# A new hand-written order table for a two-layer attention and gated-MLP kernel: zero products chained and fewer, MLP loads queued behind the query-weight transposes

## The chip, the cores and the metric

The kernel runs on one core of one Trainium2 chip. The metric is the device time of one execution in microseconds. Three timed runs of the kernel before gave 378.32, 379.09 and 379.13 us; the median, 379.09 us, is the number that the change is measured against.

## The reference, cut to what matters

`x` is 2048 x 512 in bfloat16. Two identical layers follow each other; each is an attention block with a softmax feature map instead of a softmax over positions (32 heads of 16), and then an MLP whose gate is rectified.

```python
def _A_ref(x, wqkv, w_phi, wo):
    q, k, v = split_heads(x @ wqkv)                          # 32 heads x 16
    pq, pk = q @ w_phi, k @ w_phi                            # per head
    phi = lambda p: concat([softmax(p), softmax(-p)])        # 32 features
    kv, z = phi(pk).T @ v, sum over positions of phi(pk)
    o = (phi(pq) @ kv) / (phi(pq) @ z + 1e-6)
    return merge_heads(o) @ wo
def _B_ref(x, W_gate, W_up, W_down):                         # 512 -> 1376 -> 512
    gate = x @ W_gate
    return (gate * (gate > 0) * (x @ W_up)) @ W_down
for layer in range(2):
    x = x + _A_ref(layernorm(x), ...)
    x = x + _B_ref(layernorm(x), ...)
```

The point that shapes the schedule: `kv` and `z` are sums over all 2048 positions, so no position's attention output can start before the keys of every position are done.

## The kernel before, in words

The 2048 rows are 16 tiles of 128, in four chunks of four. x stays in SBUF (tile `X`) and is updated in place; the output goes out tile by tile at the end.

**Start.** SP issues the loads of X tiles 0 and 1 (`LOAD_SP`); ACT issues the feature weights `wf`, the key half of `wkv`, X tiles 2 to 7 and the value half (`LOAD_ACT`), and later X tiles 8 to 15 and the query weights `wq` (`LATE`, L226 to L234). The MLP's and the output projection's weights (`st.loads`, L213 to L218) are 28 loads on SP (L238). `wake` (L250) issues products of a zero tile on TensorE (PE, line L256); nothing reads their results. `feature_weights` (L260) folds the per-head matrix `w_phi` into the key weights (PE transposes at L289, PE products at L302, evacuations at L245 or L247) and into the query weights. The query weights are transposed by two DMA transposes that SP issues (L275), which wait for `wq`.

**Per tile, attention.** `Norm` (L308 on) makes the layernorm: DVE statistics (L326, L328), small POOL operations (L334, L336, L384, L386), the normalised tile on ACT, POOL or DVE (L398, L410), then its transpose, either on PE (L419) with an evacuation, or by a DMA transpose on SP (L424 for two tiles, L428 for one). `keys_values` (L635 on) does, per tile: four PE products with the folded key weights (L648, called "k" below), two exponentials on ACT (L669), four PE products for the values (L601, "v") and an evacuation (L245 or L247); sums of the exponentials on DVE, partly halved first on POOL (L617, L620, L626, L630), a reciprocal (L678), the scaling of the features split between POOL and DVE (L683), and eight small PE products that add the tile to `kv` (L706, "s"). When all 16 tiles are added, `build_R` (L728, DVE, two operations) makes the matrix R. `queries` (L735 on) does the same for the queries (L748, "q"; ACT L752; DVE L757; POOL or DVE L761, L768; DMA transpose L770). The queries of the first three chunks do not need R; those of the fourth wait for the sums (`gate` is 3). `attention` (L775 on) multiplies by R on PE (L787, "a"), divides on DVE (L805, L807), transposes (PE L827 or SP) and projects with `wo` (L838, "p"), and DVE adds to X (L504).

**Per chunk, MLP.** `glu` (L513 on) has gate and up products (L551, "g", with the remainder columns at L531), ACT and DVE for the gating (L557, L561, L564, L568), and the products with `wd` (L583, "d"), which DVE adds to X (L508). In the first layer every tile that is finished goes through `Norm` again and through `keys_values` of the second layer.

**What sets the order.** Every operation is first recorded by `pl.op`, and gets a number in the order of recording. Then `Plan.order` takes the operations in the sequence of the table `ORDER`, and each engine executes its own operations strictly in that sequence. The durations and arrival times written beside an operation (`at`, `lat`, `WK_IN`, `X_IN`) are for the table's maker; they emit nothing. Inside `reads` and `writes`, a key that is not a buffer (such as `("wqin", 0)`) only demands that the table has the one operation behind the other; the waits on the chip come from the data that the instructions touch. So the table decides three things: the sequence of each engine, the sequence of SP's and ACT's DMA issues, and which buffer an operation gets. `STEP` holds the choices per tile: which engine evacuates, normalises or scales (A is ACT, D is DVE, P is POOL).

Decoded, TensorE's sequence in the table of before begins so (z is a zero product, w and wq the folding of the key and query weights, n a PE transpose of a normalised tile, the number behind a letter the tile; "0" for the layer is left out):

```
zx11 wx4 n0 w zx2 wx3 clear z n1 zx3 k0 k1 zx2 n2 v0 n3 k2 z k3 v2 n6 n7 v1 v3 n4 n5 k6 wq k4
v5 k5 wqx2 k7 wq k8 k9 zx2 q4 q0 s0 v4 q1 q6 s0 v6 v8 z s1 k11 q11 s2 v7 s3x2 k10 s4 q2 s5 k13
v13 s5 s6 q3 v11 k14 k15 v14 s7 v15 v9 k12 s7 v10 s8 v12 s8 q7 q5 q8 s9x2 s10 s11 q10 s11 s12
s13 s14x2 s15 q13 z a0 z q15 z p0 a1 q12 p0 p1 q9 a2 ...
```

and around the passage to the second layer (a digit 1 ahead of the colon is that layer):

```
... 1:k10 1:v2 1:v1 d15 d12 d14 d13 1:q6 1:v3 1:s0x2 1:v6 1:s1x2 1:k15 1:v10 1:v7 1:v5 1:v9 1:k12
1:v4 1:k14 1:s2 1:k13 1:s3x2 1:v8 1:v12 1:s4x2 1:s5x2 1:s6x2 1:s7 1:v15 1:v13 1:s7 1:v11 ...
```

SP's sequence begins: one load of `wu`, the two transposes of `wq`, the transposes of X tiles 8 and 9, then seven loads, and so on.

Of the kernel before, what the change touches and what calls it, by code (L numbers as in the profile page):

```python
# [121 lines left out]
WF_IN, WK_IN, WV_IN, WQ_IN, LOADED = 3.5, 5.92, 10.8, 14.7, 13.0  # L122
X_IN = [3.25, 4.0] + [8.06] * 2 + [9.5] * 4 + [12.1] * 4 + [13.4] * 4
# [102 lines left out]
def load_weights(st):  # L226

    nc, seen = st.nc, {}
    st.pl.rank("xl")
    before = ()  # L230
    for what, issue in st.late:
        keys = [("wqin", 0)] if what == "q" else [("Xin", t) for t in range(*what)]
        st.pl.op("ACT", 0.45, issue, reads=list(before), writes=keys, at=3.6, lat=2.0)
        before = keys[:1]  # L234
    for n, (name, dst, src, kb) in enumerate(st.loads):
        i = seen[name] = seen.get(name, -1) + 1
        st.pl.rank("ld" if name == "wd" else "l", n)
        st.pl.op("SP", 0.475, lambda dst=dst, src=src: nc.sync.dma_start(out=dst, in_=src), writes=[(name, i)], at=LOADED, lat=2.2, tx=kb / 245.0)  # L238
# [11 lines left out]
def wake(st):  # L250

    nc, pl = st.nc, st.pl
    pl.rank("z")
    for i in range(STEP["wake"]):
        z = Buf("ps", [P, D], F32)
        pl.op("PE", 0.2155, lambda z=z: nc.tensor.matmul(z[:], lhsT=st.zero[:, 0:P], rhs=st.zero[:], start=True, stop=True),  # L256
              writes=[(z, 0)], at=1.2)


def feature_weights(st):  # L260
# [8 lines left out]
    for name, dst, off, at in (("Wk2", st.Wk2, D, WK_IN), ("Wq2", st.Wq2, 0, WQ_IN)):  # L269
        pl.rank("w" if off else "wq")  # L270
        by_dma = not off
        if by_dma:
            wt = [Buf("b2", [P, 2, NDB, P], BF16) for m in range(2)]
            for m in range(2):
                pl.op("SP", 1.34, lambda m=m: nc.sync.dma_start_transpose(  # L275
                    out=wt[m][:].rearrange("p m b c -> p (m b) c"), in_=st.wq[:, 2 * m:2 * m + 2, :].rearrange("p m d -> p (m d)")),
                    reads=[("wqin", 0)], writes=[(wt[m], 0)], at=at, lat=1.88)
# [317 lines left out]
def values(st, t, ti, xnT, L):  # L595
# [7 lines left out]
    pl.op("PE", 4 * MM, mm, reads=[(xnT, ti)], writes=[(vp, 0)], at=WV_IN, group=("v" + L, t))  # L603
# [131 lines left out]
def queries(st, c, xnT, L, after=()):  # L735
    nc, pl = st.nc, st.pl
    pT = []
    for ti in range(TPC):
        t = c * TPC + ti
# [11 lines left out]
        for s in range(2):  # L751
# [10 lines left out]
              reads=[(sq2, 0), (sq2, 1)], writes=[(rq, 0)], port=not by_pool)  # L762
# [12 lines left out]
def attention(st, c, pT, norm, L):  # L775
# [73 lines left out]
    "turn": "DAADDAAD", "wake": 26, "fuse0": "AFAA", "fuse1": "FFFF", "gate": 3, "sA": 3, "xB0": "ADAADDDADDDAAAAA",  # L849
# [162 lines left out]
```

## Time and profile before

| | |
|---|---|
| three timed runs | 378.32, 379.09, 379.13 us; median 379.09 us |
| the profiled execution | 380.21 us |
| its span, first to last instruction | 378.5 us |
| what lies around the span | 1.71 us |
| mean granted TensorE clock | 0.995 |
| busy: PE, PEld, DVE, ACT, POOL | 369.6, 197.4, 263.8, 211.0, 137.5 us |

PEld is the loading of weights into TensorE, which goes on beside the products. A line of a timeline gives start, duration, engine, line, operation, output and input tile, and count; in square brackets stands how long the engine stood idle before it, and what ended that wait. A line of a table by stretches gives the stretch, its length, the busy time of each engine with the number of instructions, the granted TensorE clock (1.00 is full speed), the busy share of the DMA engines and GB/s. A line of the chain of waits gives start, duration and what. All times are microseconds from the start of the span. Buffer numbers are left out of tile names, so `ps` is any of the six PSUM buffers and `b` any of the SBUF work buffers.

### The profile page before, as it was taken

The page shows a single profiled execution, that of the slowest core. Times are in us where ns is not written, and L with a number is a line of the kernel's source. Part 1 is how long each engine was busy: PE and PEld are TensorE (multiplying, and loading weights), DVE is VectorE, ACT ScalarE, POOL GpSimd, SP SyncE. Part 2 cuts the span into 40 slices and gives each one's busy share as a digit, 9 for nine tenths or more (in the row PEclk, how much of TensorE's full clock was granted, in tenths as well). Part 3 has the DMA queues.
Part 4 walks back from the last instruction along what each step waited for, and adds up shares of the span by engine and source line. Part 5 has one row for each costly group of instructions (what it writes and reads, how often), then busy time and mean ns, then how long its engine had stood idle before and what let it go on. Part 6 is the DMA issues. An engine that isn't in the chain of part 4 may idle for free.

```text
span 378.5 us, 6950 instructions
## 1 busy us (share of the span) xinstructions
PE 369.6 (98%) x2536; PEld 197.4 (52%) x2536; DVE 263.8 (70%) x610; ACT 211.0 (56%) x476; POOL 137.5 (36%) x223
## 2 busy tenths in 40 slices
PE   7999998999999999999999999999999999999996
PEld 3454545867655444444444446476555544444453
DVE  6998998999896695535585876899846535434432
ACT  4999995967657525865587175686531342232100
POOL 5899996453330005410745257245200100100000
PEclk9999998999999999999999999999999999999999
DMA  8766385659864203600250062157851513201021
GB/s 273 178 172 140 86 206 122 130 92 142 119 136 71 57 8 65 133 5 2 56 99 0 5 100 38 29 103 136 156 84 55 72 40 44 70 0 16 0 66 61
DMA packets 95746, 31.83 MB, mean 84 GB/s; under 512 B 87424, under 2 KB 95200, under 8 KB 95712
## 3 DMA queue, kind: packets, MB, share of 16 engines
q1 hardware_dynamic: 93024, 27.97, 38.5%
q10 hardware_dynamic: 2688, 3.42, 2.6%
q8 instruction: 20, 0.33, 0.4%
q14 instruction: 14, 0.11, 0.1%
HBM read 8.44 MB, written 2.10 MB: 28 GB/s over the span
## 4 chain that ended last, share of the span: by engine, by line
PE 82%; DVE 8%; POOL 5%; DMA 3%; issue 1%; ACT 0%; ACTq 0%; POOLq 0%
PE ps L551 37%; PE ps L583 20%; PE ps L838 7%; PE ps L748 5%; PE ps L648 3%; PE ps L531 3%; PE q L787 2%; PE ps L601 2%; DVE b L683 2%; POOL b L683 2%; DMA wkv<-in_A_wqkv_dram 1%; DVE sk L630 1%; DMA b<-b 1%; POOL b L617 1%; PE q L706 1%
## 5 line engine op out<-in xcount | busy, mean ns | idle before, releaser
L551 PE MATMUL ps<-b,wg 128*128 128x512 bf16 (+3 forms) x440 | 81.8, 321 | 0.0
L551 PE MATMUL ps<-b,wu 128*128 128x512 bf16 (+3 forms) x440 | 81.3, 321 | 0.0
L561 ACT ACTIVATE b<-ps 128x512 bf16<-128x512 f32 (+3 forms) x110 | 50.4, 484 | 54.5 <-PE ps L551 53.5
L583 PE MATMUL ps<-wd,b 128*128 128x512 bf16 (+4 forms) x374 | 79.1, 366 | 0.0
L564 DVE SCALAR_TENSOR_TENSOR b<-ps,b 128x512 bf16<-128x512 f32 (+2 forms) x60 | 34.1, 593 | 32.4 <-PE ps L551 17.1
L583 PEld LDWEIGHTS <-b 128*128 128x128 bf16 (+1 forms) x374 | 35.5, 98 | 39.5
L551 PEld LDWEIGHTS <-wg 128*128 128x128 bf16 x440 | 38.8, 98 | 31.7
L551 PEld LDWEIGHTS <-wu 128*128 128x128 bf16 x440 | 38.0, 98 | 29.2
L683 POOL TENSOR_TENSOR b<-b,rk 128x1024 bf16<-128x1024 bf16 (+6 forms) x26 | 37.2, 1443 | 22.3 <-ACT sq L486 12.7
L617 POOL TENSOR_TENSOR b<-b 128x256 f32<-128x256 bf16 x39 | 26.9, 695 | 39.0 <-ACT b L752 23.0
L669 ACT ACTIVATE b<-ps 128x512 bf16<-128x512 f32 x64 | 36.8, 640 | 7.5 <-PE ps L648 6.8
L752 ACT ACTIVATE b<-ps 128x512 bf16<-128x512 f32 x64 | 35.1, 617 | 10.2 <-PE ps L748 6.8
L748 PE MATMUL ps<-Wq,b 128*128 128x512 bf16 x128 | 32.7, 386 | 0.0
L648 PE MATMUL ps<-Wk,b 128*128 128x512 bf16 x128 | 32.0, 379 | 0.3 <-DMA b<-b 0.3
L838 PE MATMUL ps<-wo,b 128*128 128x512 bf16 x128 | 32.2, 379 | 0.0
L601 PE MATMUL ps<-wkv,b 128*128 128x512 bf16 x128 | 31.2, 379 | 0.0
L504 DVE SCALAR_TENSOR_TENSOR X<-ps,X 128x512 bf16<-128x512 f32 x32 | 21.7, 684 | 10.0 <-PE ps L838 9.6
L508 DVE SCALAR_TENSOR_TENSOR X<-ps,r,X 128x512 bf16<-128x512 f32 (+2 forms) x22 | 15.1, 700 | 18.2 <-PE ps L583 18.2
L486 ACT ACTIVATE sq<-b 128x512 bf16<-128x512 bf16 x32 | 20.3, 633 | 13.5 <-DVE b L465 13.1
L490 POOL TENSOR_SCALAR ve<-tot 128x4 f32<-128x4 f32 x8 | 1.9, 233 | 65.0 <-ACT sq L486 65.0
L568 DVE TENSOR_TENSOR b<-b,b 128x128 bf16<-128x128 bf16 (+2 forms) x50 | 16.7, 361 | 11.5 <-ACT b L557 7.2
L557 ACT ACTIVATE b<-ps 128x128 bf16<-128x128 f32 (+2 forms) x50 | 20.6, 428 | 6.8 <-PE ps L551 6.1
(94 smaller groups left out, 507.1 us busy)
## 6 DMA issues: line engine op xcount, KB each, us to landing
out_dram<-X SPq DMA_DIRECT2D x15, 128.0 KB, 1.8
X<-in_A_x_dram ACTq DMA_DIRECT2D x3, 512.0 KB, 6.9
b<-b SPq DMA_TRANSPOSE x91, 3.1
wu<-in_B_W_up_dram SPq DMA_DIRECT2D x8, 160.0 KB, 4.1
wd<-in_B_W_down_dram SPq DMA_DIRECT2D x5, 256.0 KB, 4.3
wg<-in_B_W_gate_dram SPq DMA_DIRECT2D x8, 160.0 KB, 3.5
wkv<-in_A_wqkv_dram ACTq DMA_DIRECT2D x2, 512.0 KB, 6.4
wq<-in_A_wqkv_dram ACTq DMA_DIRECT2D x1, 512.0 KB, 4.8
```

What stands on the lines that cost most here:

```text
L551: nc.tensor.matmul(ps[:], lhsT=wt[:, b, f * P:(f + 1) * P], rhs=xnT[:, lo:hi, b, :], start=(b == 0), stop=(b == NDB - 1))
L561: pl.op("ACT", 0.045 + 0.43 * share, lambda ups=ups, ru=ru, sign=1.0 if fuse else -1.0: nc.scalar.activation(out=ru[:], in_=ups[:], func=A ...
L564: pl.op("DVE", 0.058 + 0.548 * share, dur=0.138 + 0.548 * share, fn=lambda gps=gps, ru=ru, h=h, cs=cs: nc.vector.scalar_tensor_tensor(out= ...
L583: nc.tensor.matmul(yps[:], lhsT=hs[f][:fsz, ti * P:(ti + 1) * P], rhs=st.wd[:fsz, f, cols], start=(f == 0), stop=(f == NFT - 1))
L601: nc.tensor.matmul(vp[:], lhsT=xnT[:, ti, kb, :], rhs=st.wkv[:, kb, D:2 * D], start=(kb == 0), stop=(kb == NDB - 1))
L617: nc.gpsimd.tensor_tensor(out=h[:].rearrange("p j h f -> p j f h"), in0=x[:, :, 0], in1=x[:, :, 1], op=Alu.add)
L648: nc.tensor.matmul(ps[:], lhsT=xnT[:, ti, kb, :], rhs=w(kb), start=(kb == 0), stop=(kb == NDB - 1))
L669: pl.op("ACT", 0.48, lambda s=s, ek=ek, pk=pk: nc.scalar.activation(out=ek[:, :, s, :], in_=pk[:].rearrange("p (j x) -> p j x", j=8), func ...
L683: eng.tensor_tensor(out=phiK[:, lo:hi, :, :].rearrange("p j s (f h) -> p (j s) f h", h=4), in0=ek[:, lo:hi, :, :].rearrange("p j s (f h) - ...
L748: nc.tensor.matmul(pq[:], lhsT=xnT[:, ti, kb, :], rhs=st.Wq2[:, kb, :], start=(kb == 0), stop=(kb == NDB - 1))
L752: pl.op("ACT", 0.48, lambda s=s, eq=eq, pq=pq: nc.scalar.activation(out=eq[:, :, s, :], in_=pq[:].rearrange("p (j x) -> p j x", j=8), func ...
L838: nc.tensor.matmul(yps[:], lhsT=turned(b), rhs=st.wo[:, b, :], start=(b == 0), stop=(b == NDB - 1))
```

## The change

The 28 weight loads move into a function of their own, which is recorded after `feature_weights`; each now has the key of the second query-weight transpose among its reads, so in any table they stand behind both transposes. The zero products are 20 instead of 26; each reads the key of the one before it, and the value products of the first four tiles read the key of the last, so that all zero products stand ahead of them. The transposed tile 0 of the first layernorm is evacuated by ACT instead of DVE (`turn`), and in `xA` (the norm ahead of the second layer) tiles 0, 7 and 10 go from DVE to ACT and tiles 2 and 8 from ACT to DVE. The estimates of arrival times are new, and one flag for the table's maker (`long`) is set on a POOL operation. The table `ORDER` is new.

```diff
-WF_IN, WK_IN, WV_IN, WQ_IN, LOADED = 3.5, 5.92, 10.8, 14.7, 13.0
-X_IN = [3.25, 4.0] + [8.06] * 2 + [9.5] * 4 + [12.1] * 4 + [13.4] * 4
+WF_IN, WK_IN, WV_IN, WQ_IN, LOADED = 3.5, 5.95, 10.0, 14.1, 13.0
+X_IN = [3.27, 3.85] + [7.2] * 2 + [8.5] * 4 + [11.4] * 4 + [12.8] * 4
...
+def later_loads(st):
+
+    nc, seen = st.nc, {}
     for n, (name, dst, src, kb) in enumerate(st.loads):
         i = seen[name] = seen.get(name, -1) + 1
         st.pl.rank("ld" if name == "wd" else "l", n)
-        st.pl.op("SP", 0.475, lambda dst=dst, src=src: nc.sync.dma_start(out=dst, in_=src), writes=[(name, i)], at=LOADED, lat=2.2, tx=kb / 245.0)
+        st.pl.op("SP", 0.475, lambda dst=dst, src=src: nc.sync.dma_start(out=dst, in_=src), reads=[("turned", 1)], writes=[(name, i)], at=LOADED, lat=2.2, tx=kb / 245.0)
...
-              writes=[(z, 0)], at=1.2)
+              reads=[("z", i - 1)] if i else [], writes=[(z, 0), ("z", i)], at=1.2)
...
-                    reads=[("wqin", 0)], writes=[(wt[m], 0)], at=at, lat=1.88)
+                    reads=[("wqin", 0)], writes=[(wt[m], 0), ("turned", m)], at=at, lat=1.88)
...
-    pl.op("PE", 4 * MM, mm, reads=[(xnT, ti)], writes=[(vp, 0)], at=WV_IN, group=("v" + L, t))
+    pl.op("PE", 4 * MM, mm, reads=[(xnT, ti)] + ([("z", STEP["wake"] - 1)] if L == "0" and t < 4 else []), writes=[(vp, 0)], at=WV_IN, group=("v" + L, t))
...
-    "turn": "DAADDAAD", "wake": 26, "fuse0": "AFAA", "fuse1": "FFFF", "gate": 3, "sA": 3, "xB0": "ADAADDDADDDAAAAA",
-    "xB1": "DDAAAAAAAADDDDAD", "xA": "DDAADDDDAADDADAD", "xm0": "11222111", "xmB0": "12221222", "xmB1": "22121122",
+    "turn": "AAADDAAD", "wake": 20, "fuse0": "AFAA", "fuse1": "FFFF", "gate": 3, "sA": 3, "xB0": "ADAADDDADDDAAAAA",
+    "xB1": "DDAAAAAAAADDDDAD", "xA": "ADDADDDADAADADAD", "xm0": "11222111", "xmB0": "12221222", "xmB1": "22121122",
...
+    later_loads(st)
```

The table's numbers are not comparable line by line, because the numbering moves: the loads are 3 to 30 before and 156 to 183 after, the first layernorm 31 to 135 before and 3 to 107 after, the zero products 136 to 161 before and 108 to 127 after, the folding 162 to 189 before and 128 to 155 after, and all the rest is 6 lower after. Decoded, TensorE's new sequence is

```
zx11 wx5 zx2 wx3 z n0 zx2 n1 zx2 k0 k1 n2 zx2 v0 clear k2 n3 v2 n6 v3 n4 n5 k3 n7 k4 wq k6 v1
wqx2 k5 wq k7 k9 v4 q0 v7 v5 q4 s0 k8 q1 s0 s1 q6 k10 v6 v8 q2 s2 s3 q3 k11 s3 k13 s4 s5x2 s6
s7 v9 k14 s7 s8x2 v11 v10 k15 v15 q11 k12 q10 v12 s9x2 v14 s10 v13 q5 q7 q8 s11x2 s12 s13
s14x2 s15 q13 a0 q15 p0 a1 q12 p0 p1 q9 a2 ...
```

and around the passage to the second layer

```
... d15 d14 1:v9 d12 1:v2 d13 1:v3 1:v6 1:s1 1:k15 1:v5 1:s1 1:v8 1:v4 1:k12 1:v11 1:k13 1:s2
1:s3x2 1:s4x2 1:v12 1:k14 1:s5x2 1:v13 1:v10 1:s6x2 1:s7 1:v15 1:s7 1:s8 1:v14 1:s9 ...
```

SP begins with the two transposes of `wq`, two loads, the transposes of X tiles 8 and 9, and four loads; at the passage it issues the DMA transposes of tiles 15, 12, 13, 14 (before: 15, 12, one of a query, 14, 13). ACT issues the load of `wq` behind the evacuations of tiles 0 and 1 (before: ahead of that of tile 1). On DVE's queue, 109 operations end with the last feature scaling of the first layer, where there were 111: the evacuation of tile 0 and one reciprocal of the queries (L757) are no longer among them. On POOL's queue, the operations up to its last such scaling are 66 instead of 67 (one L617 of the queries is behind it).

More of the change, by code (lines that the diff above doesn't have):

```diff
@@ L226, in load_weights @@
 def load_weights(st):
-    nc, seen = st.nc, {}
+    nc = st.nc
     st.pl.rank("xl")
@@ L761, in queries @@
               lambda sq2=sq2, rq=rq, e=nc.gpsimd if by_pool else nc.vector: e.tensor_tensor(out=rq[:], in0=sq2[:, :, 1, :], in1=sq2[:, :, 0, :], op=Alu.mult),
-              reads=[(sq2, 0), (sq2, 1)], writes=[(rq, 0)], port=not by_pool)
+              reads=[(sq2, 0), (sq2, 1)], writes=[(rq, 0)], port=not by_pool, long=by_pool)
         on_dve = STEP["qs" + L][t] == "D"
```

144 rows, old and new, of the table ORDER are left out of this document.

## The prediction

> **What bounds the kernel now.** I read the busy shares first, then the same by stretches of the run.
>
> ```profile
> PE 369.6 (98%) x2536; PEld 197.4 (52%) x2536; DVE 263.8 (70%) x610; ACT 211.0 (56%) x476; POOL 137.5 (36%) x223
> 20.00:30.00 10.00, 10.00 (x66) 5.10 (x64) 9.76 (x24) 10.00 (x22) 9.60 (x14) 1.00 0.75 188
> 55.57:58.98 3.41, 1.65 (x29) 1.02 (x28) 3.41 (x6) 2.45 (x6) 2.69 (x4) 1.00 0.67 210
> 58.98:62.40 3.42, 3.42 (x23) 1.74 (x24) 2.04 (x6) 1.04 (x2) 1.67 (x3) 0.50 0.71 165
> 64.00:216.60 152.60, 152.60 (x1010) 82.78 (x1007) 112.24 (x280) 96.71 (x239) 52.69 (x95) 1.00 0.40 71
> 216.60:240.00 23.40, 22.71 (x227) 12.50 (x226) 16.69 (x33) 13.63 (x26) 13.16 (x16) 1.00 0.34 58
> 240.00:375.70 135.70, 135.56 (x870) 71.72 (x867) 77.08 (x170) 49.05 (x115) 16.52 (x27) 1.00 0.33 63
> ```
>
> 98% for TensorE hides two regimes. Behind 64 us TensorE has no gap worth a name: whatever time the attention starts earlier, the end comes earlier, and whatever a new order makes it wait is added. Ahead of that DVE (9.76), ACT (10.00) and POOL (9.60 of 10.00 at 20 to 30) are as full as TensorE, and from 55.57 TensorE does 1.65 us of work in 3.41, while DVE is full. The chain of waits and the timeline say who leads there.
>
> ```profile
> 38.42 4.19 POOL L683 TENSOR_TENSOR b<-b,rk 128x768 bf16<-128x768 bf16 x3
> 56.01 2.89 DVE b L683 x3
> 58.94 0.62 PE L706 MATMUL q<-vext,b 128*128 128x68 bf16 x8 [0.81 <-DVE b L683]
> 59.38 1.90 PE L748 MATMUL ps<-Wq,b 128*128 128x512 bf16 x4
> 59.60 0.79 DVE L728 TENSOR_TENSOR R<-M,q 128x272 bf16<-128x272 bf16 x2
> 61.07 0.63 PE L256 MATMUL ps<-zero 128*128 128x512 bf16 x1
> 61.50 0.66 PE L787 MATMUL q<-R,b 128*128 128x68 bf16 x8
> 61.96 0.59 PE L256 MATMUL ps<-zero 128*128 128x512 bf16 x1
> 62.19 0.36 DVE L805 RECIPROCAL dd<-q 128x32 f32<-128x32 f32 x1 [1.26 <-PE q L787]
> 62.59 0.69 DVE L807 TENSOR_TENSOR b<-q,dd 128x512 bf16<-128x512 f32 x1
> 63.26 0.38 PE L256 MATMUL ps<-zero 128*128 128x512 bf16 x1
> 63.47 0.39 PE L827 MATMUL ps<-ident,b 128*128 128x128 bf16 x4
> 205.54 1.73 PE ps L601 x8
> ```
>
> POOL and then DVE scale the last keys (L683), TensorE adds them (L706), DVE builds R from 59.60 to 60.39. The first attention product could start then; it starts at 61.50, because one query group (L748, at half clock: 59.38 to the next start, 61.07, so 1.69; a full-speed group of four takes 0.865, half of the 1.73) and a zero product (61.07 to 61.50, 0.43) stand ahead of it. Three zero products lie on this path.
>
> **The change part by part.** *R.* Two instructions fewer stand on DVE's full queue ahead of the last scaling: tile 0's evacuation and one reciprocal.
>
> ```profile
> L247 DVE COPY b<-ps 128x512 bf16<-128x512 bf16 x7 | 2.6, 417 | 1.4 <-PE ps L289 1.2 <-PE ps L419 0.3
> L757 DVE RECIPROCAL sq<-sq 128x32 f32<-128x32 f32 x32 | 10.7, 339 | 0.1
> ```
>
> That is 0.417 + 0.339 = 0.76 us; POOL, the other full queue, has one L617 fewer there, so it follows. ACT takes the evacuation over, some 0.6 us, beside exponentials that it has to make anyway; if ACT leads in the first 20 us, half of the gain is gone. I take R 0.76 earlier, at 58.84.
>
> *The early load.* One load of `wu` no longer runs beside the key weights, whose arrival starts the work.
>
> ```profile
> 1.71 0.42 SPq L238 DMA_DIRECT2D wu<-in_B_W_up_dram  x1
> 6.79 1.07 PE L289 MATMUL ps<-ident,wkv 128*128 128x128 bf16 x16 [1.47 <-DMA wkv<-in_A_wqkv_dram]
> 5.00:6.00 1.00, 0.32 (x2) 0.00 (x0) 0.97 (x5) 0.00 (x0) 0.92 (x3) 1.00 1.09 368
> ```
>
> Its 160 KB at 368 GB/s are 0.43 us of engines that are full. How much of it lay ahead of the key weights the trace doesn't show: 0 to 0.43. I take 0, since the load was issued last of the three on SP; 0.43 goes into the range. The Trainium skill, DMA: Bandwidth & Descriptors, section Queues, rings and completion order, says that each DMA engine alternates between the queues packet by packet, so that SP's load would take turns with ACT's; the full DMA share in the row agrees, and by the rule alone the sum would be up to 0.43 better.
>
> *The other loads.* All 28 wait behind the transposes of `wq`, as 27 did before.
>
> ```profile
> 14.26 2.71 SPq L275 DMA_TRANSPOSE b<-wq  x2
> 59.52 0.45 SPq L238 DMA_DIRECT2D wu<-in_B_W_up_dram  x1
> wu<-in_B_W_up_dram SPq DMA_DIRECT2D x8, 160.0 KB, 4.1
> 69.22 0.61 PE L551 MATMUL ps<-b,wu 128*128 128x128 bf16 x8
> ```
>
> The last one was issued at 59.52 and landed some 4.1 later, at 63.6; the MLP starts at 69.22. The 5.6 us of cover make later issues free, also if `wq`, now issued behind two evacuations, comes a microsecond later and holds SP. Behind the waiting transposes stand only loads and the transposes of tiles 8 and 9, issued at 21.00 before. Cost 0; without cover, one for one.
>
> *The zero products.* Nine instead of 12 lie between 6.79 and R; these three stood in a stage that DVE and POOL bound, so I take 0, between 0 and 3 x 0.22 = 0.65. The three behind R go: the one at 61.07 gives 0.43. The other two stand where TensorE waits for DVE to divide: from 61.50 to the transpose at 63.47 are 1.97 us. Without them the path is the product 0.25, L805 0.36, L807 0.69 and handovers as before, from about 1.3 up to 1.9 at half clock. I take 0.3 of gain, between 0.1 and 0.6.
>
> *The clock.* 58.98 to 62.40 ran at half. If TensorE is as idle ahead of R as before, it will again: the 3.41 us ahead hold 1.65 of work, and the new order has the same sums behind the last early query. The work ahead of R is shorter by three zero products but so is the time. I take it as recurring; at full clock the query group ahead of the first attention product would give another 1.69 - 0.865 = 0.82.
>
> *The passage to layer 2.* Here the new table thins the cover of one chain.
>
> ```profile
> 216.82 0.75 DVE L508 SCALAR_TENSOR_TENSOR X<-ps,r,X 128x512 bf16<-128x512 f32 x1 [0.58 <-PE ps L583]
> 217.60 0.69 DVE L326 BATCH_NORM_STATS2 bnst<-X 128x6 f32<-128x512 bf16 x1
> 218.34 0.17 DVE L328 BATCH_NORM_AGGREGATE mv<-bnst 128x2 f32<-128x6 f32 x1
> 219.11 1.09 POOL L336 TENSOR_TENSOR rstd<-ve,mhalf 128x1 f32<-128x1 f32 x2
> 219.72 0.41 DVE L410 TENSOR_SCALAR b<-X,mv,rstd 128x512 bf16<-128x512 bf16 x1 [1.20 <-POOL rstd L336]
> 220.55 0.81 ACT L398 ACTIVATE b<-X,ve,rstd 128x512 bf16<-128x512 bf16 x1 [1.79 <-POOL ve L386]
> 221.39 2.50 SPq L428 DMA_TRANSPOSE b<-b  x2
> 220.47 1.69 POOL L683 TENSOR_TENSOR b<-b,rk 128x896 bf16<-128x896 bf16 x1
> 222.67 4.59 DMA b<-b
> 227.31 1.04 PE L648 MATMUL ps<-Wk,b 128*128 128x512 bf16 x4 [0.27 <-DMA b<-b]
> b<-b SPq DMA_TRANSPOSE x91, 3.1
> ```
>
> Tile 13 is the last of layer 1. From its last product (216.8) to the arrival of its transpose (222.67 + 4.59 = 227.26) are 10.5 us, covered but for 0.27. In the new table only eight groups of four and eight small products stand between: 8 x 0.865 + 0.25 = 7.2 us. But the chain shortens. Before, tile 13 was normalised at 220.13 (219.72 + 0.41) and its transpose stood on SP behind tile 14's, which waited for ACT; now SP issues 13 ahead of 14. By the rows: 0.75 + 0.69 + 0.17 + 0.2 (POOL) + 0.55 (half of L336's 1.09) + 0.41 is 2.8, handovers 0.5, and 3.1 to 4.6 for the transpose: 6.4 to 7.9. So a wait of 0 to 0.7 where 0.27 stood: I take 0.
>
> *Behind 64 us.* No gap before, so the order has nothing to win but 0.69 (23.40 - 22.71), and each wait costs its length. I take 0, between +0.7 and -2.
>
> **Sum.** 0.76 + 0.43 + 0.3 = 1.5 us. The profiled execution is 380.21, its span 378.5 with 1.71 around it, so 378.7 profiled; the profiled one lies 1.12 over the median of 379.09. I predict **377.6 us**.
>
> **The rivals.**
>
> 1. *The clock stays up.* For it: the 0.50 depends on where the 3.41 us fall, and the runs of before are 0.8 apart. Against: nothing in the new order fills TensorE ahead of R. It gives 379.09 - 1.5 - 0.8 = 376.8. The Trainium skill, TensorE: Matmul & The Clock Gate, section Why this matters for your kernels, asks for no idle gaps over about 3 us; by it the halving should not come at all. The trace does not agree: the longest wait of TensorE there is 0.81 us, and the clock fell.
> 2. *Tile 13's keys wait* (slower). On POOL the 128x896 scaling of tile 10 (1.69), behind the small operations of tiles 13 and 14 before, now stands ahead of tile 13's. If it starts late, it adds its whole length to a chain of up to 7.9; with the latency of before, 10.5, TensorE stands for 10.5 - 7.2 = 3.3 us more: 379.09 - 1.5 + 3.3 - 0.27 = 380.6. It decides the sign from a wait of about 1.8 us, a latency of 9.0.
> 3. *The zero products were padding and R is no earlier.* DVE's two instructions go into waits for ACT, and the early stage runs as before: 379.09 - 0.3 = 378.8. For it: POOL and ACT are full too at 20 to 30.
>
> **How the numbers follow.** Forecast 0.36, rival 1 0.24, rival 2 0.22, rival 3 0.12; 0.06 for a sum with all upper ends: 1.5 + 0.82 + 0.43 + 0.65 + 0.3, so 375.4. A measurement of this kernel tells about 0.2%, 0.76 us, from no change. Faster: forecast, rival 1 and the upper ends, less some for the ends at which they fall within (0.04): 0.62. Same: rival 3 and a share of rival 2, 0.16. Slower: 0.22. The range goes from 375.4 to 380.6.
>
> **What would show it.** R (L728) starting at about 58.8 and the first L787 within 1.7 us of it would show the first two terms; a granted clock of 0.5 in the 3.41 us around R would show the third, 1.00 rival 1. In the passage, the wait of L648 for the DMA: under 1 us by me, over 2 by rival 2. The start of L289 tells what the early load cost. Wrong would be: new waits of TensorE behind 64 us that sum to over 1 us, or R later than 59.6 because ACT leads.

## The result, and the profile after

The changed kernel takes 377.92 us (median of nine executions, 377.31 to 378.53) beside 379.13 us for the kernel before: a ratio of 0.9968, 95% interval 0.9954 to 0.9982, so 0.3% faster. The prediction was 377.6. The number is right, and in part by luck: two terms that make up half of the sum are worth nothing, and of the 1.2 us measured here 0.5 to 0.9 is left between the medians at full clock.

The profiled execution of after took 377.86 us, with a span of 376.1 and a clock of 0.999. These are its rows for the stretches read before: busy times of PE, PEld, DVE, ACT and POOL, granted clock, DMA share, GB/s.

```profile
20.00:30.00 10.00, 10.00 (x65) 5.11 (x63) 10.00 (x24) 10.00 (x22) 9.62 (x15) 1.00 0.93 201
55.57:58.98 3.41, 2.60 (x45) 1.62 (x43) 3.41 (x9) 2.21 (x6) 2.18 (x4) 1.00 0.00 0
58.98:62.40 3.42, 3.04 (x30) 1.65 (x31) 3.29 (x9) 3.22 (x7) 3.14 (x8) 1.00 0.56 106
...
214.20:237.60 23.40, 23.15 (x223) 12.49 (x222) 17.09 (x33) 13.33 (x25) 13.80 (x18) 1.00 0.23 43
237.60:373.30 135.70, 135.11 (x866) 71.29 (x864) 76.43 (x169) 49.73 (x115) 16.66 (x27) 1.00 0.32 65
```

The clock is 1.00 around R, where before showed 0.50, and ahead of R TensorE works 2.60 of 3.41 us instead of 1.65. DVE is now full from 20 to 30 us as well (10.00, before 9.76). Behind 214 us the gaps sum to 0.25 + 0.59 = 0.84 where 0.69 + 0.14 = 0.83 stood. The timelines of TensorE and DVE around R:

```profile
57.45 0.43 PE L711 MATMUL q<-vext,b 128*128 128x68 bf16 x8 [0.33 <-DVE b L688]
57.72 1.02 PE L753 MATMUL ps<-Wq,b 128*128 128x512 bf16 x4
59.04 0.41 PE L792 MATMUL q<-R,b 128*128 128x68 bf16 x8 [0.29 <-DVE R L733]
59.29 1.02 PE L753 MATMUL ps<-Wq,b 128*128 128x512 bf16 x4
60.63 0.40 PE L832 MATMUL ps<-ident,b 128*128 128x128 bf16 x4 [0.32 <-DVE b L812]
60.87 0.42 PE L792 MATMUL q<-R,b 128*128 128x68 bf16 x8
```

```profile
57.32 0.34 DVE L762 RECIPROCAL sq<-sq 128x32 f32<-128x32 f32 x1
57.58 0.62 DVE L635 TENSOR_REDUCE sq<-b 128x32 f32<-128x512 bf16 x1
58.13 0.77 DVE L733 TENSOR_TENSOR R<-M,q 128x272 bf16<-128x272 bf16 x2
```

The code lines have moved by five: L733 was L728 (R), L792 was L787 (attention), L753 was L748 (queries), L711 was L706 (sums), L843 was L838. R starts at 58.13 instead of 59.60, and the first attention product 0.91 behind it instead of 1.90. TensorE now waits 0.29 for R itself, where a zero product stood, and 0.32 for DVE's division (L812), where the last of the three stood.

The passage to the second layer went as I had reckoned. Tile 13's last product, its normalisation and its key products are these:

```profile
217.13 0.75 DVE L513 SCALAR_TENSOR_TENSOR X<-ps,r,X 128x512 bf16<-128x512 f32 x1 [0.44 <-PE ps L588]
...
219.98 0.41 DVE L415 TENSOR_SCALAR b<-X,mv,rstd 128x512 bf16<-128x512 bf16 x1 [0.67 <-POOL rstd L341]
```

```profile
224.49 1.04 PE L653 MATMUL ps<-Wk,b 128*128 128x512 bf16 x4 [0.23 <-DMA b<-b]
```

From 217.1 to 224.49 are 7.4 us where 10.5 stood (I had 6.4 to 7.9), and the wait is 0.23 where it was 0.27. POOL's 128x896 scaling started at 217.13, early enough, so rival 2 did not come.

**The profiled execution of before was not a typical one.** Each execution lists its mean granted clock. Of 109 further executions of the kernel before, 23 show 0.995, as the profiled one did, and 86 show 0.999 or 1.000 (two more, of 554 and 1380 us, are left out). The 23 are longer, by 1.1 to 1.9 us between the medians of the two kinds on the three chips. So a second profile of before, at full clock, stands beside after below.

### The profile page after: what moved, and what is told of

Same layout as the page of the kernel before. It is cut to its first block, busy times and chain, and to the rows that moved or that the text cites. A ratio compares the mean times of both kernels' runs of the same rounds, so it can differ in the third digit from the quotient of the medians.

```text
span 376.1 us, 6927 instructions
## 1 busy us (share of the span) xinstructions
PE 368.5 (98%) x2530; PEld 196.6 (52%) x2530; DVE 262.5 (70%) x608; ACT 212.5 (57%) x478; POOL 136.5 (36%) x223
## 4 chain that ended last, share of the span: by engine, by line
PE 83%; DVE 12%; ACT 1%; DMA 1%; POOL 1%; issue 1%
PE ps L556 37%; PE ps L588 20%; PE ps L843 7%; PE ps L753 4%; PE ps L653 4%; PE ps L536 3%; PE ps L606 3%; DVE b L688 3%; PE q L792 2%; DVE sk L625 2%; DVE rk L683 2%; PE ps L261 1%; DVE sk L635 1%; DMA b<-b 1%; PE q L711 1%; DVE bnst L331 1%
## 5 line engine op out<-in xcount | busy, mean ns | idle before, releaser
L757 ACT ACTIVATE b<-ps 128x512 bf16<-128x512 f32 x64 | 37.3, 642 | 8.9 <-PE ps L753 7.6
L674 ACT ACTIVATE b<-ps 128x512 bf16<-128x512 f32 x64 | 37.7, 645 | 5.9 <-PE ps L653 5.4
L843 PE MATMUL ps<-wo,b 128*128 128x512 bf16 x128 | 32.7, 379 | 0.0
L753 PE MATMUL ps<-Wq,b 128*128 128x512 bf16 x128 | 32.0, 379 | 0.0
L573 DVE TENSOR_TENSOR b<-b,b 128x128 bf16<-128x128 bf16 (+2 forms) x50 | 15.0, 332 | 14.8 <-ACT b L562 9.8
L773 POOL TENSOR_TENSOR b<-b,rq 128x512 bf16<-128x512 bf16 x21 | 22.1, 1056 | 0.7
L812 DVE TENSOR_TENSOR b<-q,dd 128x512 bf16<-128x512 f32 x32 | 21.8, 683 | 0.6
```

What stands on the lines that cost most here:

```text
L674: pl.op("ACT", 0.48, lambda s=s, ek=ek, pk=pk: nc.scalar.activation(out=ek[:, :, s, :], in_=pk[:].rearrange("p (j x) -> p j x", j=8), func ...
L753: nc.tensor.matmul(pq[:], lhsT=xnT[:, ti, kb, :], rhs=st.Wq2[:, kb, :], start=(kb == 0), stop=(kb == NDB - 1))
L757: pl.op("ACT", 0.48, lambda s=s, eq=eq, pq=pq: nc.scalar.activation(out=eq[:, :, s, :], in_=pq[:].rearrange("p (j x) -> p j x", j=8), func ...
L843: nc.tensor.matmul(yps[:], lhsT=turned(b), rhs=st.wo[:, b, :], start=(b == 0), stop=(b == NDB - 1))
```

## The experiments

**The kernel before again** (unchanged; label before_again).

> The kernel before, unchanged, so that its trace can be read at full clock. Theory (the profiled execution of before was one of the few in which the clock halves around R; at full clock R of before starts at 59.0 as in the runs that keep its front): span 377.0 +/- 0.3, clock 1.00, R at 59.0 to 59.1, first attention product at 59.95 to 60.5, and, since the work arrives about 1.5 us sooner than in the halved execution, a wait of L838 for a DMA transpose of 0.3 to 0.7 us between 245 and 262 where the halved execution had none. Rival (the halved execution is typical and the front-keeping runs were sped up by their edits): R at 59.6, no wait of L838.

Median 379.1 us, ratio to the other runs of before 1.000 (0.998 to 1.002). Its profile has a span of 377.3 and a clock of 1.00. TensorE around R:

```profile
58.84 0.43 PE L706 MATMUL q<-vext,b 128*128 128x68 bf16 x8 [0.81 <-DVE b L683]
59.10 1.02 PE L748 MATMUL ps<-Wq,b 128*128 128x512 bf16 x4
59.96 0.38 PE L256 MATMUL ps<-zero 128*128 128x512 bf16 x1
60.23 0.41 PE L787 MATMUL q<-R,b 128*128 128x68 bf16 x8
60.49 0.38 PE L256 MATMUL ps<-zero 128*128 128x512 bf16 x1
...
61.83 0.40 PE L827 MATMUL ps<-ident,b 128*128 128x128 bf16 x4
62.06 0.42 PE L787 MATMUL q<-R,b 128*128 128x68 bf16 x8
```

```profile
59.30 0.79 DVE L728 TENSOR_TENSOR R<-M,q 128x272 bf16<-128x272 bf16 x2
```

R is done at 59.30 + 0.79 = 60.09, and the attention product starts at 60.23, 0.93 behind the start of R; in after this is 0.91. The zero product at 59.96 lies in the wait for R. From the first attention product to the second are 1.83 us here and 1.83 in after. **At full clock the zero products behind R cost nothing**; my 0.43 and 0.3 came from rows at half clock. R itself is at 59.30, not at the 59.0 that the theory expected, because the key weights came late in this execution: 1.73 us of wait, as its row below shows. The wait of L838 is 0.3.

**The changed kernel again** (unchanged; label after_again, on the same chip as the one above).

> The changed kernel, unchanged, beside the others of this set on one chip. Theory (gain of the front, no halving of the clock): 1.0 +/- 0.4 us under before, ratio 0.997, clock 1.00 in all executions, R at 58.1 to 58.3. Rival (the 0.3% was the chip on which it was measured): ratio 0.999 or above.

Median 378.1 us, ratio 0.9978 (0.9960 to 0.9997); no execution with a lowered clock. R at 58.46, first attention product at 59.37. So the gain repeats, though smaller; the intervals of the two measurements overlap. R came a little later than expected, again because of the key weights. First the start of the key-weight transposes of before at full clock, then that of this run:

```profile
6.87 1.07 PE L289 MATMUL ps<-ident,wkv 128*128 128x128 bf16 x16 [1.73 <-DMA wkv<-in_A_wqkv_dram]
```

```profile
6.52 1.07 PE L294 MATMUL ps<-ident,wkv 128*128 128x128 bf16 x16 [0.67 <-DMA wkv<-in_A_wqkv_dram]
```

This start lies between 5.91 and 6.87 in the profiles of this case, and R follows it. In all 14 it comes 0.04 to 0.09 us behind the landing of the key weights; in after, new_front and a_turn_D the timeline shows no wait there, because zero products run up to it. To compare orders, count from it. All columns are read from the timelines; the last is the span less the start of the first attention product of the second layer.

| profile | front | rest | key weights' transposes | R | between | R to first attention product | second layer's first to end |
|---|---|---|---|---|---|---|---|
| before (half clock at R) | old | old | 6.79 | 59.60 | 52.81 | 1.90 | 140.8 |
| before_again | old | old | 6.87 | 59.30 | 52.43 | 0.93 | 141.3 |
| b_load_late | old | old | 6.47 | 59.05 | 52.58 | 0.94 | 141.5 |
| b_no_z3 | old | old | 6.03 | 58.60 | 52.57 | 0.94 | 142.3 |
| new_rest | old | new | 6.38 | 59.02 | 52.64 | 0.93 | 140.8 |
| new_front | new | old | 6.17 | 58.15 | 51.98 | 0.90 | 141.7 |
| nf_z3 | new | old | 6.07 | 58.02 | 51.95 | 0.90 | 141.5 |
| after | new | new | 5.91 | 58.13 | 52.22 | 0.91 | 141.0 |
| after_again | new | new | 6.52 | 58.46 | 51.94 | 0.91 | 140.6 |
| a_z3_back | new | new | 6.27 | 58.23 | 51.96 | 0.91 | 141.0 |
| a_z11 | new | new | 6.59 | 58.41 | 51.82 | 0.92 | 141.2 |
| a_load_early | new | new | 6.53 | 58.52 | 51.99 | 0.90 | 141.0 |
| a_turn_D | new | new | 6.04 | 58.20 | 52.16 | 0.91 | 141.4 |
| a_14_first | new | new | 6.09 | 58.07 | 51.98 | 0.91 | 141.1 |

From key weights to R the old front takes 52.43 to 52.64 at full clock (mean of four 52.56), the new one 51.82 to 52.22 (mean of nine 52.00): 0.56 us, and the two groups do not touch.

**The two halves of the table.** First the new sequence up to R with before's order and `xA` behind it (new_front), then before's up to R with the new order behind it (new_rest). Of before's three zero products behind the last sums new_rest keeps the one ahead of the first attention product and leaves out the other two.

```diff
-ORDER = the table of after
+ORDER = table of after up to build_R + table of before for all the rest    (new_front)
+ORDER = table of before up to build_R + table of after for all the rest    (new_rest)
```

> The new table up to and with R of the first layer (its loads, its 20 zero products, ACT evacuating tile 0), and everything behind R in the sequence of before. Theory (the gain is made ahead of the first attention product, the rest is neutral): 1.2 us faster than before, 0.8 to 1.6, and the first L787-type product at about 59.0. Rival (the reordering behind 64 us makes the gain): within 0.4 us of before.

> The opposite half: the sequence of before up to R with its early load of wu and its zero products, the new sequence behind it, so without the two zero products behind R. Theory: within 0.4 us of before, at best 0.4 faster from the two zero products. Rival (the reordering behind 64 us makes the gain): 1.2 us faster.

new_front: 377.63 us, ratio 0.9966 (0.9947 to 0.9984). new_rest: 378.32 us, ratio 0.9992 (0.9977 to 1.0007). The front alone carries as much as the whole change; the rest alone cannot be told from nothing. In the profile of new_front a wait stands that neither profile of after has (engine, line, releaser; sum, times, longest):

```profile
PE ps L843 <- DMA b<-b: 0.8, 1, 0.8
```

It is the projection of the second layer's attention, at 250 us, waiting for a DMA transpose on SP. The last column points the same way: 141.3 to 142.3 with the old rest at full clock, 140.6 to 141.4 with the new one, in the mean 0.7 (0.5 if the first profile of before, 140.8, is counted as well: its half clock lies ahead of this stretch). The medians do not bear this out: with the new front, the old rest gives 377.63 and, with three zero products (nf_z3 below), 378.17, the new rest 377.92 and 378.1.

**Parts of the change undone, and one done alone.** The load of `wu` put back ahead of the transposes in after (a_load_early), and the same load put behind them in before (b_load_late):

```diff
-... reads=[("turned", 1)], writes=[(name, i)], at=LOADED ...
+... reads=[("turned", 1)] if n != 20 else [], writes=[(name, i)], at=LOADED ...
 ORDER: that load (176; 23 before) moved ahead of the two DMA transposes of wq (a_load_early), behind them (b_load_late)
```

> The changed kernel with one load of wu (160 KB) moved back to the head of SP's queue, where it was before. Theory (the early load delays the key weights): L294-type transposes start at 6.8 instead of 5.9, 0.5 to 0.9 us slower than the changed kernel. Rival: the start is later but the time the same within 0.3 us.

> The kernel before with one table entry moved: the load of wu that SP issued at 1.71 stands behind the two transposes of wq. Theory: the key weights land about 0.9 us earlier (L289 at 5.9 instead of 6.79), the whole early stage follows, 0.5 to 0.9 us faster. Rival (DVE, ACT and POOL bind the stage, so an earlier start is used up in waits): L289 earlier, but within 0.3 us of before.

a_load_early: 378.26 us, ratio 0.9977 (0.9965 to 0.9989). b_load_late: 378.65 us, ratio 1.0002 (0.9984 to 1.0019). Done alone the edit gives nothing; the transposes started at 6.47, not at the 5.9 that was expected. In a_load_early they started at 6.53 (6.8 expected). Undone, it leaves a ratio within the interval of after_again (0.9978). The transposes of the key weights start at 6.52 in the mean of five profiles with the early load and at 6.24 in that of nine without; the groups overlap by most of their width (6.03 to 6.87 and 5.91 to 6.59), so a gain of up to 0.3 is possible and not shown.

Tile 0's evacuation given back to DVE (a_turn_D):

```diff
-    "turn": "AAADDAAD", ...
+    "turn": "DAADDAAD", ...
```

> The changed kernel with tile 0 of the first layernorm evacuated by DVE again, at the same place of the table. Theory (DVE leads to R): R 0.4 us later and 0.2 to 0.5 us slower than the changed kernel. Rival (ACT leads the early stage): the same or up to 0.3 us faster.

378.26 us, ratio 0.9979 (0.9966 to 0.9992). Key weights to R 52.16, inside the new front's own 51.82 to 52.22. Of the 0.42 us that this instruction takes, some 0.2 shows in R, counted against the mean of the other eight new fronts (51.98).

**The zero products.** The three behind R taken out of before (b_no_z3); three put into after at those places (a_z3_back); the same in new_front (nf_z3); and after with only its first 11 (a_z11).

```diff
-... lambda z=z: nc.tensor.matmul(z[:], ...)
+... lambda z=z, i=i: None if i in (18, 20, 22) else nc.tensor.matmul(z[:], ...)      (b_no_z3)
+... lambda z=z, i=i: None if i in (11, ..., 19) else nc.tensor.matmul(z[:], ...)     (a_z11)
-    "wake": 20
+    "wake": 23, and in ORDER the three ahead of a0, behind a0, behind q15              (a_z3_back, nf_z3)
```

> The kernel before without its three zero products behind the last sums of layer 1 (they were the entries at 61.07, 61.96 and 63.26); nothing else moves. Theory: 0.3 to 0.7 us faster, one product of 0.22 to 0.43 ahead of the first attention product and part of the other two. Rival (they fill waits for DVE): within 0.2 us. Second rival (they hold the clock up): slower, with more than 3.4 us at a granted clock of 0.5.

> The changed kernel with three zero products put back at their old places behind the last sums: ahead of the first attention product, behind it, and behind the next query group. Theory: 0.3 to 0.5 us slower than the changed kernel (0.22 for the first, part of the second, none of the third). Rival: no difference within 0.2, as they stand in waits.

> The new front up to R with the order of before behind it, and before's three zero products behind R at their old places (the earlier run of new front and old rest had none). Theory (they stand in TensorE's waits for DVE; what is won ahead of 240 us is given back in the wait of L843 for the DMA transposes at 247 to 260): same as new front without them, 377.6 to 377.9, and the wait of L843 shorter by what the zero products take, 0.1 to 0.5 instead of 0.8. Rival (each costs its 0.22 to 0.43, as I predicted): 0.4 to 0.7 us slower than new front alone, 378.2.

> The changed kernel with only the first 11 of its 20 zero products: the 9 between the first weight transposes and the first value product aren't issued. Theory (that stage is bound by DVE, POOL and ACT, the zero products stand in TensorE's waits, so they cost nothing): R within 0.1 us of the changed kernel's, 58.0 to 58.3, time within 0.3 us of it. Rival 1 (they are on the path): R up to 9 x 0.22 = 2 us earlier, at least 0.4. Rival 2 (they hold the clock up): without them the granted clock falls to 0.5 for a window of 3.4 us in the first 60 us, and the time is 0.5 to 2 us longer in some executions.

| | us | ratio to before (95%) |
|---|---|---|
| b_no_z3 | 379.38 | 1.0017 (1.0001 to 1.0033) |
| a_z3_back | 377.66 | 0.9961 (0.9946 to 0.9976) |
| nf_z3 | 378.17 | 0.9972 (0.9955 to 0.9989) |
| a_z11 | 377.95 | 0.9967 (0.9949 to 0.9985) |

Taking them out of before does not gain; it is a little slower. Putting them in is once a little faster than the kernel without them, once a little slower (new_front 0.9966), all within the intervals. The 378.17 of nf_z3 is close to what its rival gave (378.2), but the difference from new_front is not made behind R: from R to the first MLP product both profiles take 8.26 us. The column "R to first attention product" is the same with and without them. The nine between the first weight transposes and the first value product cost nothing either: from the key weights to R a_z11 takes 51.82, at the lower end of the others (R itself, at 58.41, is later than the 58.0 to 58.3 expected, since the key weights landed late), and TensorE waits instead, for ACT's evacuations:

```profile
PE ps L653 <- ACT b L250: 1.3, 2, 1.1
```

Why b_no_z3 is slower is settled only in part. Up to the second layer its profile agrees with before's at full clock (0.94 and 0.93; 168.5 and 168.4 us from the first MLP product to that layer's first attention product). Behind it, L838 waits twice for SP's transposes:

```profile
250.94 1.90 PE L838 MATMUL ps<-wo,b 128*128 128x512 bf16 x8 [0.68 <-DMA b<-b]
...
260.25 1.90 PE L838 MATMUL ps<-wo,b 128*128 128x512 bf16 x8 [0.47 <-DMA b<-b]
```

The first wait ends with the landing of a transpose of the attention's output (L814; L819 in the new front). The chain of waits shows it, first in b_no_z3, then in new_front:

```profile
246.49 4.41 DMA b<-b
```

```profile
245.55 4.51 DMA b<-b
```

The three transposes that SP issues right behind it are stretched as well. First b_no_z3, then before at full clock:

```profile
247.81 4.87 SPq L477 DMA_TRANSPOSE b<-b  x3
```

```profile
248.44 3.84 SPq L477 DMA_TRANSPOSE b<-b  x3
```

In new_front they take 5.06, in b_load_late 3.85; the excess is all in the first of the three (2.25 instead of 1.22 in b_no_z3).

The DMA records of the traces show what goes with it. Between 245.7 and 248.2, one packet of 16 KB starts on a DMA queue of the kind "instruction" and takes 0.9 to 1.6 us. The landing of the L814 transpose goes with how long after its issue that packet starts. Where it starts 0.99 us or more behind (b_no_z3, new_front, nf_z3, a_z11), that transpose lands 4.3 to 4.5 us after its issue, and these four are the profiles with a wait of L838 near 250. Where it starts 0.4 to 0.9 behind, the transpose lands after 3.3 to 3.8, and where it starts earlier, after 3.1 to 3.3.

The next such packet, near 258, goes in the same way with the waits near 260 in before_again, b_load_late and b_no_z3 (landing after 4.7 to 5.1; after 4.6 in new_rest too, where the products come later and do not wait). In the first profile of before it came only at 260.09, and there was no wait. This is an order of events in the traces; no run moved the packet by itself. So the old rest stands on the edge of a wait there. (Of the profiles with the new rest, only a_z11 has a wait of this line, 0.4.) b_no_z3 waits 1.1 us in these two places and before_again 0.3; the 0.8 between them is about what the medians at full clock differ by on b_no_z3's chip (379.37 and 378.63).

**The passage, with tile 14's transpose ahead of tile 13's** (a_14_first):

```diff
 SP at the passage: DMA transposes of tiles 15, 12,
-13, 14
+14, 13
```

> The changed kernel with SP issuing the DMA transpose of tile 14 ahead of that of tile 13 at the passage to layer 2, as before. Theory (the new issue order is what lets 7.2 us of work cover tile 13's chain): tile 13's transpose is issued some 1.3 us later, the wait of 0.23 us grows to 0.8 to 2, and the time with it. Rival (there is slack in the transfers): within 0.3 us.

378.64 us, ratio 0.9984 (0.9972 to 0.9996); inside the interval of after_again, though the slowest of the kernels with the new front. The wait at the passage is 0.47 instead of 0.23:

```profile
224.94 1.04 PE L653 MATMUL ps<-Wk,b 128*128 128x512 bf16 x4 [0.47 <-DMA b<-b]
```

From the first MLP product to the second layer's first attention product it takes 169.3 us, where the seven other profiles with the new rest take 168.2 to 168.8. The order on SP is part of what shortens the chain, as the prediction said; it is worth some tenths, not the 3 us of rival 2.

None of the kernels beats the changed one by more than the intervals allow.

## Why the prediction was right in its number, and where its steps failed

**R earlier by 0.76: near in size, but not shown to come by the way that I counted.** The order gives 0.56. I counted instructions on DVE's queue, and one of the two, the evacuation, shows some 0.2 of its 0.42 (a_turn_D). DVE's rows from the key weights to R, in before at full clock and in after_again, and what DVE waits for in before there (the rows that after_again no longer has):

```profile
6.87:59.30 52.43, 50.05 (x395) 26.58 (x396) 50.41 (x106) 47.61 (x92) 48.66 (x65) 1.00 0.69 170
```

```profile
6.52:58.46 51.94, 49.72 (x393) 26.46 (x394) 50.98 (x105) 47.84 (x92) 47.99 (x65) 1.00 0.73 175
```

```profile
DVE rk L678 <- POOL b L683: 0.6, 1, 0.6
DVE sk L626 <- POOL b L617: 0.6, 2, 0.4
```

DVE works longer in after (50.98 against 50.41) and waits less (0.96 against 2.02). The two waits for POOL, 1.2 us, stand in all five profiles with the old front, and in none of the nine with the new one. Against them stand longer scalings. The five of 1024 columns, in before at full clock and in after_again:

```profile
L683 DVE TENSOR_TENSOR b<-b,rk 128x1024 bf16<-128x1024 bf16 x5 | 4.1, 844 | 0.0
```

```profile
L688 DVE TENSOR_TENSOR b<-b,rk 128x1024 bf16<-128x1024 bf16 x5 | 5.2, 1038 | 0.0
```

Same work, 5 x 0.194 = 1.0 us more; all 13 of DVE's scalings ahead of R take 9.33 us in the one and 10.47 in the other. What slows them is in the rows of POOL. The longest of after_again:

```profile
31.39 1.69 POOL L688 TENSOR_TENSOR b<-b,rk 128x896 bf16<-128x896 bf16 x1
31.76 1.87 DVE L688 TENSOR_TENSOR b<-b,rk 128x1024 bf16<-128x1024 bf16 x1
```

POOL's own scaling was running when DVE's began, and DVE's ends 0.55 us behind POOL's end (33.08 and 33.63). In all 14 traces, DVE's scalings of 1024 columns that begin while POOL runs a scaling, a halving or L761 end 0.54 to 0.55 us behind the end of that operation, whether they last 735 or 1869 ns; those that begin beside none of these last 620 to 680. I read that as DVE standing still until POOL's operation is done, while the profile counts the time as work; no run tests it. Summed over the 13 scalings, this hidden wait is 4.67 us in before at full clock and 5.77 in after_again: 1.1 us more, about what the two visible waits for POOL came to. By this account the waits have moved into the busy time and do not give the 0.56. Beyond the 0.2 of the evacuation, which part of the order gives it is not separated.

One of my two instructions was miscounted as well: the reciprocal that I took off the queue ahead of the last scaling stands behind that scaling but ahead of R (57.32 in the rows of after), so it is still on the path. The 1.47 between the profiles of before and after (59.60 to 58.13) is 0.88 from the start of the key weights' transposes (6.79 to 5.91) and 0.59 from the order; the start of R alone did not tell the two apart.

**The early load, taken as 0:** not contradicted. By the Trainium skill's rule of alternating queues (DMA: Bandwidth & Descriptors, section Queues, rings and completion order) it would be up to 0.43; the means of the profiles differ by 0.28, inside their scatter, so the runs neither bear the rule out nor speak against it.

**The other loads, 0:** held; no profile has a wait for a weight of the MLP or of the projection.

**The zero products ahead of R, 0:** held (a_z11). **Behind R, 0.43 + 0.3: failed.** The failing step is the working from the rows at 61.07 and 63.47, which I read as a path of TensorE. They stand in a half-clock stretch: the query group took 1.69 there and ended behind R. At full clock it takes 0.86 and the wait for R, and then for DVE, hides each zero product. Measured: 0.02 and 0.00. The sign that I had named for this term, a first attention product within 1.7 us of R, came (0.91), but it comes in the full-clock profiles of before as well (0.93). Rival 3 was right that the zero products are padding, and wrong that R is no earlier.

**The clock, "I take it as recurring": failed**, twice over. For before I did not weigh that a clock of 0.995 in one execution says nothing of how often it comes; it is about one in five. For after the premise was that TensorE is as idle ahead of R. The emptiest 3.41 us around R, in before at full clock and in after_again:

```profile
55.60:59.01 3.41, 1.81 (x34) 1.00 0.67 201
```

```profile
56.00:59.41 3.41, 2.54 (x47) 1.00 0.00 0
```

The old fronts have 1.65 to 1.81 us of work there, the new ones some 2.5; a_z11 alone of the new ones has an emptier stretch, at 7.4 (1.98). None of 99 executions of the eight kernels with the new front shows a lowered clock, whatever zero products they have; of the 145 of the four kernels with the old front 28 do. An emptier stretch does not bring it by itself: four profiles with the old front ran through theirs at full clock. What else decides is open. So rival 1 is what happened, but its 0.8 us is won only in the executions that lost it. The rule of the Trainium skill that I weighed there (TensorE: Matmul & The Clock Gate, section Why this matters for your kernels), no gaps over about 3 us, does not tell the two fronts apart: neither has such a gap.

**The passage, 0:** held; from the first MLP product to the second layer's first attention product are 168.4 us with the old rest and 168.5 with the new (means of five and seven profiles, a_14_first left out).

**Behind it, 0 (+0.7 to -2): perhaps missed on the good side, not shown.** In single profiles the new rest is shorter by 0.5 to 0.7 us there, since its transposes on SP stand further from the wait of L838. I read before's 135.56 of 135.70 as no gap to win; that one execution happened not to wait there (140.8 in the table), the five others with the old rest did. By medians at full clock the new rest gains 0.5 with the old front (378.63 to 378.17, though the ratio of new_rest cannot be told from 1), and nothing with the new one.

Single profiles so add up to 0.56 + 0.02 - 0.1 + 0.7 = 1.2 us in place of my 1.5, of which only the first is clear of their scatter. Between the medians at full clock it is 0.5 to 0.9 us (378.6 to 378.8 for before on three chips, 377.9 and 378.1 for after); the first set of before, at 379.13, stands above those, and the clocks of its executions are not on record. The two halves alone come to 1.0 and 0.5 below before's 378.63, more together than the whole change brings; finer than that the sum is not settled. In the chances, the 0.04 that I took from "faster" is all that "same" has beside rival 3: no share of rival 2 is in it, whose 0.22 stands under "slower".

## What to carry to other kernels

Look first at the clock of every execution: a term worked out in a stretch at half clock may not exist at full clock, where something else ends the wait. Before two traces are compared, put them on the event that starts the work, since a DMA's arrival can move everything behind it by a microsecond. On a queue that looks full, compare the length of the same instruction from one place to the next before counting instructions: a row that is three times as long as another of its size may hold a wait for a neighbour, and a wait that goes from the table of waits may only have moved there.

## What the runs showed of the hardware that was not expected

- The granted clock fell for one stretch of 3.41 us behind one in which TensorE had done 1.65 us of work, with no gap longer than 0.81 (the profiled execution of before). With that front a lowered clock came in 28 of 145 executions, with the new one, 2.54 us of work in the emptiest such stretch around R, in none of 99.
- The start of the first transposes, 0.04 to 0.09 us behind the landing of the key weights in all 14 profiles, moved by 0.96 us between them (5.91 to 6.87), and the whole front with it.
- The same three DMA transposes took 3.84 to 5.06 us of SP's queue, in the same order, and the transpose ahead of them landed 3.1 to 4.5 us after its issue; in all 14 traces the late ones go with a 16 KB packet of an instruction queue that starts 0.99 us or more behind the issue.
- A DVE scaling of 128x1024 took 620 to 1869 ns: when POOL was in a scaling or halving of its own at its start, it ended 0.54 to 0.55 us behind that one's end, in all 14 traces.
